# A DeltaNet and mixture-of-experts kernel: PSUM banks by pairs, a short product summed by VectorE, zero fills and gathers moved in the plan

## The chip, the cores and the metric

The kernel runs on one core of a Trainium2 chip. The metric is the device time of one execution in microseconds (us). The engines of the core are TensorE (PE in the profile, PEld for its weight loads), VectorE (DVE), ScalarE (ACT), GpSimd (POOL) and SyncE (SP, which here only issues transfers).

## The reference

Two blocks follow each other. The first is a DeltaNet: for each of 4 x 8 heads a state matrix of 48 x 48 is updated at each of 768 steps. The second routes each of the 3072 rows to one of 8 experts, each of which is a two-layer network.

```python
for t in range(S):                                   # S = 768, per head, D = 48
    y[t] = q[t] @ state
    v_old = k_n[t] @ state                           # k_n is k over its norm
    state = state + b[t] * outer(k_n[t], v[t] - v_old)
x = y.transpose(0, 2, 1, 3).reshape(3072, 384)
expert = argmax(x @ w_gate); gate = softmax(x @ w_gate)[expert]
out[i] = gate[i] * (relu(x[i] @ w1[expert[i]]) @ w2[expert[i]])   # w1 384 x 1024, w2 1024 x 384
```

## The kernel before

**A planner writes the order.** Each operation is registered with `P.op(engine, cost, function, r=, w=, prio=, lat=)`: its engine, an assumed cost in us, the keys that it reads and writes, a priority (smaller first) and, for transfers, an assumed latency. `Plan.order` simulates the engines with these numbers and emits all instructions in the order that it found. On the chip each engine runs its own instructions in that order; the waits between engines are set afterwards, from the tiles that the instructions really read and write. The keys of the planner are its own: PSUM is one key per bank, `("bk", b)`, while the tiles are four pairs of two banks, and bank b lies in pair b // 2.

**The attention** works in 12 chunks (`t`) of 64 steps for all heads. `load_kq(t)` brings keys and queries into a ring of six slots in `kqA`; slots are zeroed first (L332, L1069). `scores(t)` multiplies keys with keys and queries (L373); for t = 0 and 1 the results go by ScalarE (t = 0) and VectorE (t = 1) into `GD` with four copies each (L384 to L388, shown at the helper's lines L307 and L309). `invert(n)` does two chunks at a time on VectorE: two transposes (L436), the norms of the keys (L444 to L466, `nt` at L471), and then a triangular inversion of some hundred small operations. It uses `u` and `x21`, zeroed by GpSimd (L431, L432). `turn(t)` carries the state `S` (two tiles `Sbs`, zeroed at L329), `output(t)` and `logits(t)` make the rows x and their logits, and `route` and `listed` make the lists of rows for each expert (`lst`, `rows_i`) from `ents`, whose first column is a copy of constants from `cf` (L700). `last_rows` zeroes `folds` and writes it to the last rows of `xs`, the buffer of the rows x in device memory.

**The experts.** Each expert takes up to 416 rows: three tiles of 128 and a short one of 32. `early` does the first two tiles of expert 0 before the last rows are known; `expert(e)` does the rest. In each:

- `fetch(e)` gathers rows of `xs` by indirect transfers from GpSimd's queue (L879), `turned_rows` transposes them on TensorE through banks 0 and 1 (L920), and the result is evicted by VectorE (L928) or, for the middle strip, by ScalarE (L926);
- `hidden` makes the hidden layer in eight blocks f of 128 (L938, six instructions each), evicted with a relu by ScalarE for even f (L947) and VectorE for odd f (L944), through the banks given to it;
- `short` makes the second product of the short tile in four column groups (L1015, bank 5), each over two of the eight blocks. ScalarE copies the bank to `folds` (L1019), and `fold` adds the four groups with a matmul against ones (L1023, bank 6);
- `second` makes the second product of a full tile (L967, sixteen instructions), in banks 6, 7 and 5;
- `finish` scales by the gate into one of three `ys` (L955 on VectorE, L958 on ScalarE) and scatters the rows to `out` (L886). All scatters write the key `out`.

What the planner is told sets where the pieces stand: `prio` of transposes is half a step ahead of their expert, so they serve as filling work in the expert before, once their rows are expected to have landed (`lat` of the gather).

## Time and profile before

| | us |
|---|---|
| median of 3 runs (lowest, highest) | 555.9 (553.9, 559.57) |
| the profiled execution | 554.24 |
| its span in the profile | 552.5 |
| TensorE busy in it | 483.8 (88%) |
| VectorE busy | 229.9 (42%) |
| ScalarE busy | 195.5 (35%) |
| GpSimd busy | 84.8 (15%) |
| mean granted clock of TensorE | 0.943 of full |

In the rows of a view, `L967 PE MATMUL pair<-blkA,kqA 128*128 128x384 f32 x32` is line, engine, operation, tile written from tiles read, shape and count; the two numbers ahead of it in a timeline are start and length in us (a merged row has the length from its first start to its last end), and the bracket tells how long the engine had been idle and what it had waited for. Buffer numbers are left out: all four PSUM pairs are called `pair`, and `kqA` in an expert holds gathered rows, transposed rows and hidden layers, since the ring is free by then. fp32 matmuls stand as two instructions each.

### The profile page before, as it was taken

How to read it: one execution, taken by the hardware profiler on the slowest of the kernel's cores; microseconds unless marked ns; L12 is line 12 of the kernel's file. 1: busy time of each engine (PE TensorE's matmuls, PEld its weight loads, DVE VectorE, ACT ScalarE, POOL GpSimd, SP SyncE). 2: the span in 40 equal slices, each digit the busy share in tenths (PEclk: the TensorE clock that was granted, in tenths of full speed). 3: DMA queues.
4: the chain of work that ended last, by engine and by line, in shares of the span. 5: the costliest groups of instructions: out<-in, count | busy, mean ns of one | idle time of the engine just before them, and what ended most of it. 6: DMA issues, size and time to landing. Idle time of an engine off the chain costs nothing. (4 is left out here: it accounts for less than half of the span.)

```text
span 552.5 us, 15891 instructions
## 1 busy us (share of the span) xinstructions
PE 483.8 (88%) x6900; PEld 332.0 (60%) x6901; DVE 229.9 (42%) x932; ACT 195.5 (35%) x459; POOL 84.8 (15%) x91
## 2 busy tenths in 40 slices
PE   5458888778989999898999999999999999999990
PEld 3347777667778889775755555555555555545540
DVE  3999989999899651250211011010110011101100
ACT  3394979778887843410111011011110110111100
POOL 9000000000100001022420142110331102002011
PEclk9557999999999996998999999999999999999995
DMA  8966356464422451393453144412541300001000
GB/s 211 239 158 187 97 162 161 135 162 108 119 95 89 142 199 31 112 386 102 133 200 115 22 171 161 138 50 87 171 163 40 138 2 31 16 0 44 1 30 12
DMA packets 27851, 63.82 MB, mean 116 GB/s; under 512 B 4027, under 2 KB 16221, under 8 KB 27745
## 3 DMA queue, kind: packets, MB, share of 16 engines
q1 hardware_dynamic: 23376, 52.44, 31.4%
q0 software_dynamic: 3584, 9.44, 4.9%
q8 instruction: 55, 0.90, 0.7%
q10 hardware_dynamic: 816, 0.88, 0.7%
q14 instruction: 20, 0.16, 0.1%
HBM read 49.64 MB, written 11.01 MB: 110 GB/s over the span
## 5 line engine op out<-in xcount | busy, mean ns | idle before, releaser
L938 PE MATMUL pair<-kqA,blkA 128*128 128x416 f32 (+2 forms) x288 | 86.3, 457 | 0.4 <-DVE kqA L928 0.4
L967 PE MATMUL pair<-blkA,kqA 128*128 128x384 f32 x240 | 81.0, 495 | 0.0
L944 DVE TENSOR_SCALAR kqA<-pair 128x416 f32<-128x416 f32 (+2 forms) x36 | 19.6, 543 | 127.9 <-PE pair L938 80.1
L938 PEld LDWEIGHTS pair<-kqA,blkA 128*128 128x128 f32 x288 | 51.8, 190 | 32.0 <-issue 29.3
L967 PEld LDWEIGHTS pair<-blkA,kqA 128*128 128x128 f32 x240 | 45.5, 193 | 35.0 <-issue 6.4
L886 POOL DMA_INDIRECT out<-y,rows_i x30 | 28.7, 958 | 201.5 <-ACT y L958 144.6
L947 ACT ACTIVATE kqA<-pair 128x416 f32<-128x416 f32 (+2 forms) x36 | 17.2, 479 | 108.8 <-PE pair L938 79.5
L373 PE MATMUL pair<-kqA 48*64 48x128 f32 (+1 forms) x896 | 35.4, 305 | 20.2 <-ACT pA L307 12.2
L958 ACT ACTIVATE y<-pair,lst 128x384 f32<-128x384 f32 x15 | 8.7, 581 | 124.2 <-PE pair L967 109.5
L938 PE MATMUL pair<-kqA,pA 128*128 128x416 f32 x144 | 51.4, 514 | 0.0
L529 ACT ACTIVATE v<-v,nt 128x48 f32<-128x48 f32 x192 | 48.9, 330 | 1.9 <-DMA v<-in_vtok 1.9
L967 PE MATMUL pair<-pA,kqA 128*128 128x384 f32 x144 | 48.0, 490 | 0.0
L955 DVE TENSOR_SCALAR y<-pair,lst 32x384 f32<-32x384 f32 (+1 forms) x15 | 8.5, 607 | 92.3 <-PE pair L1023 92.3
L373 PEld LDWEIGHTS pair<-kqA 48*64 48x64 f32 x896 | 28.6, 162 | 26.6 <-ACT pA L307 14.1
L938 PEld LDWEIGHTS pair<-kqA,pA 128*128 128x128 f32 x144 | 27.1, 190 | 23.2 <-issue 22.6
L967 PEld LDWEIGHTS pair<-pA,kqA 128*128 128x128 f32 x144 | 26.9, 190 | 21.2 <-issue 3.8
L553 PE MATMUL pair<-S,kqA 112*64 112x96 f32 x704 | 36.1, 255 | 3.4 <-issue 1.6
L879 POOL DMA_INDIRECT kqA<-xs,rows_i x30 | 29.7, 990 | 49.3 <-DMA pA<-in_w 25.5
L553 PEld LDWEIGHTS pair<-S,kqA 112*64 112x64 f32 x704 | 31.4, 141 | 6.1 <-issue 3.8
L582 PE MATMUL pair<-R,blkA 32*32 32x48 f32 x1536 | 28.7, 223 | 4.7 <-ACT R L307 3.3
L582 PEld LDWEIGHTS pair<-R,blkA 32*32 32x32 f32 x1536 | 25.2, 146 | 8.6 <-ACT R L307 4.6
L489 DVE TENSOR_TENSOR prod<-blkA 128x16 f32<-128x16 f32 (+7 forms) x96 | 28.0, 292 | 0.0
(134 smaller groups left out, 628.6 us busy)
## 6 DMA issues: line engine op xcount, KB each, us to landing
kqA<-in_kq SPq DMA_DIRECT2D x46, 192.0 KB, 5.0
blkA<-in_w SPq DMA_DIRECT2D x15, 512.0 KB, 4.7
blkA<-in_w SPq DMA_DIRECT2D x10, 768.0 KB, 5.1
v<-in_vtok SPq DMA_DIRECT2D x12, 384.0 KB, 3.9
kt<-in_ktok SPq DMA_DIRECT2D x12, 384.0 KB, 3.6
xs<-x SPq DMA_DIRECT2D x12, 384.0 KB, 2.8
pA<-in_w SPq DMA_DIRECT2D x9, 512.0 KB, 4.9
pA<-in_w SPq DMA_DIRECT2D x6, 768.0 KB, 5.3
```

Source lines behind the costliest of these rows:

```text
L373: nc.tensor.matmul(bk[bank + e][half(x), i * w : i * w + w].rearrange("p (k c) -> p k c", c=C), lhsT=v[feat(e), 0, x * FQ + f, :], rhs=v[f ...
L489: dve(16 * w, lambda j=j, w=w, pl=pl: nc.vector.tensor_tensor(out=pl, in0=gl[:, 16:32, j : j + 1].to_broadcast([128, 16, w]), in1=u[:, j : ...
L529: P.op("ACT", 0.225, lambda v=v, i=i: nc.scalar.activation(out=v, in_=v, func=AF.Copy, scale=nt[:, 16 * u + i : 16 * u + i + 1]), r=[("nt" ...
L553: nc.tensor.matmul(bk[bank + g][half(x ^ g if first else x), 2 * D * i : 2 * D * i + 2 * D], lhsT=KQ(t)[0 : 64 + D, k, x * FQ + f, :], rhs ...
L582: nc.tensor.matmul(at(BZ, f, e)[quad(q)], lhsT=tt[quad(q), :, 16 * u + 8 * e + f], rhs=R[quad(q), f, e, :], start=True, stop=True, skip_gr ...
L879: nc.gpsimd.indirect_dma_start(out=dst, out_offset=None, in_=xs, in_offset=bass.IndirectOffsetOnAxis(ap=idx, axis=0), bounds_check=N - 1, ...
L886: nc.gpsimd.indirect_dma_start(out=out, out_offset=bass.IndirectOffsetOnAxis(ap=idx, axis=0), in_=src, in_offset=None, bounds_check=N - 1, ...
L938: nc.tensor.matmul(bk[b][:, 0:n], lhsT=a1[:, s, f * 128 : f * 128 + 128], rhs=xT[:, s, :], start=(s == 0), stop=(s == NK - 1))
L944: (lambda f=f, b=b: nc.vector.tensor_scalar(out=hT[:, f, :], in0=bk[b][:, 0:n], scalar1=0.0, scalar2=None, op0=OP.max))
L947: (lambda f=f, b=b: nc.scalar.activation(out=hT[:, f, :], in_=bk[b][:, 0:n], func=AF.Relu)),
L958: (lambda: nc.scalar.activation(out=y[0:n], in_=bk[b][0:n, 0:DM], func=AF.Copy, scale=gate)),
L967: nc.tensor.matmul(bk[b][:, 0:DM], lhsT=hT[:, f, at : at + 128], rhs=a2[:, f, :], start=(f == 0), stop=(f == NF - 1))
```

## The change

The memsets of `Sbs`, of ring slot 0 and of `folds` are registered after the first inversion and read its `nt` in the plan; so do the memsets of `u` and `x21` for the second inversion. The copy into `ents` goes from VectorE to ScalarE, with another priority. The gathers are planned with a latency of 5.0 instead of 2.5 us. `hidden` gets banks that alternate between two pairs, so that ScalarE's blocks lie in one pair and VectorE's in the other, and the second products of a full expert use banks 6, 1 and 7. `short` writes bank 2; the fold and ScalarE's copy are taken out, and VectorE scales the first of the four column groups into y and adds the other three to it, scaled, after which y is scattered at once. The planner then finds another order for the experts' stage.

```diff
-    for i in range(2):
-        P.op("POOL", 1.4, lambda i=i: nc.gpsimd.memset(Sbs[i][:], 0.0), w=[("S", i, e) for e in range(2)], prio=-15)
...
+        past = [("nt", 0)] if n == 1 else []
+        P.op("POOL", 0.9, lambda: nc.gpsimd.memset(u, 0.0), r=past, w=[ku, (*ku, 21)], prio=pr - 1)
+        P.op("POOL", 0.3, lambda: nc.gpsimd.memset(x21[:], 0.0), r=past, w=[kx], prio=pr - 1)
...
-    dve(24, lambda: nc.vector.tensor_copy(out=ents[:, :, 0], in_=const("numbers")), ["cf"], ["ents"], -2)
+    P.op("ACT", 0.15, copy("ACT", ents[:, :, 0], const("numbers")), r=["cf"], w=["ents"], prio=2)
...
-                 r=["rows_i", *allx], w=[("xin", e % 2, t)], prio=30 + e, lat=2.5)
+                 r=["rows_i", *allx], w=[("xin", e % 2, t)], prio=30 + e, lat=5.0)
...
-        hidden(0, xT, hT, 21, guard, (0, 1, 4, 5))
+        hidden(0, xT, hT, 21, guard, (0, 4, 1, 5))
         for t in range(2):
-            second(0, t, hT, 128 * t, 6 + t, 21.2 + 0.01 * t)
+            second(0, t, hT, 128 * t, (6, 3)[t], 21.2 + 0.01 * t)
...
-        hidden(e, xT, hT, pr, guard, (2, 3, 4))
+        hidden(e, xT, hT, pr, guard, (2, 4, 3, 5))
...
-        P.op("PE", 1.6, short, r=hk, w=[("bk", 5)], prio=pr + 0.3, passes=16, use=1536)
-        P.op("ACT", 0.5, lambda: nc.scalar.activation(out=folds[:], in_=bk[5][:, 0:DM], func=AF.Copy),
-             r=[("bk", 5)], w=["folds"], prio=pr)
-
-        def fold():
-            nc.tensor.matmul(bk[6][0:32, 0:DM], lhsT=const("fold"), rhs=folds[:], start=True, stop=True)
+        P.op("PE", 1.6, short, r=hk, w=[("bk", 2)], prio=pr + 0.3, passes=16, use=1536)
...
+        gate, idx = col(3)
+        y, ky = next_y()
+        for c in range(4):
+            part = bk[2][32 * c : 32 * c + 32, 0:DM]
+            P.op("DVE", 0.55, (lambda y=y, part=part: nc.vector.scalar_tensor_tensor(
+                out=y[0:32], in0=part, scalar=gate[0:32], in1=y[0:32], op0=OP.mult, op1=OP.add))
+                if c else (lambda y=y, part=part: nc.vector.tensor_scalar(
+                    out=y[0:32], in0=part, scalar1=gate[0:32], scalar2=None, op0=OP.mult)),
+                r=[("bk", 2), "lst"], w=[ky], prio=pr + 0.35)
+        P.op("POOL", 1.0, lambda y=y: scatter(y[0:32], idx[0:32]), r=[ky, "rows_i"], w=["out"], prio=pr + 0.35, lat=2.5)
+
         for i, t in enumerate(tiles):
-            if i == len(tiles) - 1:
-                P.op("PE", 0.8, fold, r=["folds", "cf"], w=[("bk", 6)], prio=pr + 0.41, passes=2, use=200)
-                gate, idx = col(3)
-                finish(True, 6, 32, gate[0:32], idx[0:32], "rows", pr + 0.4)
-            b = (6, 7, 5)[i]
+            b = (6, 1, 7)[i] if e else 7
             second(e, t, hT, 128 * i, b, pr + 0.4 + 0.01 * i)
             finish(i % 2, b, 128, *col(t), "rows", pr + 0.4)
...
-    last_rows()
...
+            if i == 2:
+
+                for j in range(2):
+                    P.op("POOL", 1.4, lambda j=j: nc.gpsimd.memset(Sbs[j][:], 0.0), r=[("nt", 0)],
+                         w=[("S", j, e) for e in range(2)], prio=-15)
+                P.op("POOL", 1.85, lambda: nc.gpsimd.memset(kqA[:, 0:2048], 0.0), r=[("nt", 0)],
+                     w=kKQ(0) + [("zero", 0)], prio=0)
+                last_rows()
```

## The prediction

> **What bounds the kernel now.** I read the busy rows of the page first: TensorE is busy 88% of the span, no other engine over 42%.

> ```profile
> PE 483.8 (88%) x6900; PEld 332.0 (60%) x6901; DVE 229.9 (42%) x932; ACT 195.5 (35%) x459; POOL 84.8 (15%) x91
> ```

> That is an average over two stages. The table of 25 us windows separates them: from 25 to 175 us VectorE is busy 22.4 to 24.9 us of each 25 (the inversions bound the attention), and from 275 to 525 us TensorE is busy 24.3 to 25.0 of 25 at a granted clock of 1.00. So the head matters through VectorE's chain, the experts through each TensorE instruction and gap, and the last few us through whatever follows the last product. I then read the timeline in four places.

> In an expert (timeline of all engines):

> ```profile
> 447.89 10.59 PE L967 MATMUL pair<-blkA,kqA 128*128 128x384 f32 x32
> 458.52 0.58 ACT L958 ACTIVATE y<-pair,lst 128x384 f32<-128x384 f32 x1 [10.00 <-PE pair L967]
> 459.15 0.83 PE L1023 MATMUL pair<-folds,cf 128*32 128x384 f32 x2 [0.67 <-ACT y L958]
> 459.92 5.43 PE L967 MATMUL pair<-blkA,kqA 128*128 128x384 f32 x16
> ```

> The x32 are two second products, in banks 6 and 7, both in pair 3. ScalarE's y is bank 6's, done half-way, yet it starts after both: an eviction here waits for every earlier write to its pair. The fold wants bank 6, so TensorE waits.

> At the end (same view):

> ```profile
> 535.69 0.98 POOL L886 DMA_INDIRECT out<-y,rows_i  x1 [2.38 <-DMA out<-y,rows_i]
> 538.40 0.58 ACT L958 ACTIVATE y<-pair,lst 128x384 f32<-128x384 f32 x1 [6.33 <-PEq L1112]
> 539.06 0.88 POOL L886 DMA_INDIRECT out<-y,rows_i  x1 [2.40 <-DMA out<-y,rows_i]
> 542.01 0.97 POOL L886 DMA_INDIRECT out<-y,rows_i  x1 [2.07 <-DMA out<-y,rows_i]
> ```

> Scatters run one at a time, each after the transfer of the one before. The last y is ready at 538.98, but the short tile's scatter (0.88) stands ahead of it.

> In the middle, two windows (columns: stretch, its length, busy us of PE, PEld, DVE, ACT, POOL, granted clock, DMA share, GB/s), and from the timeline the wait that they show:

> ```profile
> 248.00:252.00 4.00, 0.89 (x5) 0.78 (x5) 0.42 (x1) 0.39 (x1) 3.08 (x4) 0.87 0.89 305
> 252.00:254.00 2.00, 2.00 (x5) 1.14 (x4) 0.33 (x1) 0.30 (x1) 1.58 (x2) 0.50 0.32 98
> ```
> ```profile
> 251.25 1.09 PE L920 MATMUL pair<-cf,kqA 128*128 128x128 f32 x4 [3.11 <-DMA kqA<-xs,rows_i]
> ```

> TensorE stands 3.11 us for a gather, and then has half its clock for 2 us.

> At the head:

> ```profile
> 6.53 3.44 ACT L307 ACTIVATE blkA<-pair 32x512 f32<-32x512 f32 x5 [2.35 <-PE pair L373]
> 10.34 4.55 DVE L700 COPY ents<-cf 128x24 f32<-128x24 f32 x1 [7.58 <-DMA cf<-c_f]
> 10.43 6.57 DVE L309 COPY blkA<-pair 32x512 f32<-32x512 f32 x4
> 14.44 0.41 POOL L905 MEMSET folds<- 128x384 f32 x1
> 17.11 1.30 DVE L436 STREAM_TRANSPOSE blkA<-blkA 128x512 f32<-128x512 f32 x2
> ```

> VectorE waits for the constants, then a copy of 24 elements takes 4.55 us: it ends at 14.89, when GpSimd's run of zero fills (the last 14.44 + 0.41) is over. The four L309 queue behind it, and L436, first of the inversion, behind them.

> **The change, part by part**, against the profiled execution, 554.24 us (span 552.5 and 1.74 around it).

> *The fold goes.* From the first product's start to the third's is 12.03 us (447.89 to 459.92; 12.02 for experts 5 and 7). The 32 instructions alone are 10.59 − 5.43 = 5.16 us for 16, so 10.32. The fold with its wait costs 1.71 us; in expert 0, where it stands between two hidden chunks, 274.19 to 285.31 is 11.12, less 12 × 0.349 + 5.16: 1.77. Eight experts: 13.7. The fourth L1015 bank now goes to VectorE: one scale and three adds at 0.60 (row of L955 on 32x384), 2.4 us, beside the 5.16 us product that follows, in which VectorE has nothing else. ScalarE loses its folds copy (0.49), hidden before too. **−13.7.**

> *Banks alternate between pairs.* In `hidden` TensorE waits nowhere now (0.4 us in all at L938), so nothing is gained there. The early expert's second product moves to pair 1, which VectorE empties beside the transposes that follow. f and f+2 share a pair, but a chunk lasts 2.1 us (6 × 0.349) and an eviction 0.52 to 0.59: hidden; without that cover each chunk would wait some 0.7. Second products in pairs 3, 0, 3 let the first y start 5.2 us earlier, beside the next product.

> *The transposes move.* In the built order of the changed kernel, four of them stand before each short product instead of eight, and the others gather after the last second product: sixteen before expert 3's hidden, twelve before 5's, eight before 7's. They share pair 0, so a group waits for the evictions of the groups ahead. Two groups, then two L928 (0.59 each) and two hand-overs of 0.1: 1.35 before experts 3 and 5, 0.8 (one eviction) before 7, and about 0.3 before 4 and 6, whose transposed strip ScalarE evicts behind a y (0.58). **+4.1.** Before expert 2 the first two strips' hidden matmuls (1.4 us) cover it. Lower bound 1 (the next strips' matmuls hide most), upper 9 (every group waits for one eviction more).

> *Gathers planned longer.* The early expert's second products now come straight after its hidden product (about 248.2), so 10.3 us of TensorE work covers the gathers, whose last issue was at 252.88. Second products to 258.5, ten transposes with one eviction wait 2.0, then hidden of expert 0, which reaches at 261.1 the place it now has at 265.30. **−4.2**: the 3.1 us wait and 1.1 of half clock. Behind the early scatter POOL now has the second one before expert 2's gathers. Later, gathers stand behind three scatters that wait for y: expert 5's behind expert 2's last. Four gathers at 1.3 each and 4.3 to land, from some 2.3 us after the last product, land 12 us after it; their first reader comes after a whole hidden product (16.8) and waits of 1.3. Cover left: 6 us. SP's order is unchanged; expert 3's weights wait for expert 0's products, which end earlier.

> *Tail.* The short scatter now goes 15 us before the last one, and products are 5.2 apart, over the 3.35 from scatter to scatter. Last y to scatter is 0.27 (532.07 to 532.34), so 539.25 instead of 542.01. **−2.8.**

> *Zeros behind the first logits.* In the built order GpSimd's instructions stand as before and the fills have no wait on nt: the added reads bind the planner alone. SP, whose copy of folds comes behind the fills, keeps its order too. Nothing.

> *ents on ScalarE.* It heads ScalarE's queue and waits for cf (10.34); behind it stand the four L307 copies and the fifth, which ran from 6.53. So: 10.34 + 0.2 + 4 × 0.59 = 12.9 (fifth 13.97; TensorE's next scores and GpSimd's last big fill wait for that, to about 15.2). On VectorE L309 no longer stands behind a copy; its matmuls are done at 7.94 (5.25 + 2.69). Does it run beside the fills? [...] Net 3.6 on VectorE; the ScalarE–TensorE chain gains 2.9 (16.3 for 19.18). Bounds 0 and 4; no row shows a PSUM copy beside a fill, but transposes at 102.17 beside one took their usual 0.70. **−3.3**, passed on, as VectorE bounds the attention.

> Sum: −13.7 + 4.1 − 4.2 − 2.8 − 3.3 = −19.9, so 534.3 on this execution. It stood 1.7 under the median of 555.9; against the median, **536**.

> **Rivals.**
> 1. *The head gives nothing*: L309 stands beside fills, or ScalarE's wait for cf eats it. For: 4.55 us for 24 elements. [...] 539.3.
> 2. *The transposes eat it*: nine evictions' wait, 9 us instead of 4.1. For: pair-wide waits, as in the expert above. Against: the next strip's matmuls. 541. With rival 1, 544.
> 3. *Gathers late (slower)*: POOL's gathers behind scatters land after TensorE wants them; each time costs what it cost at 251 us, 4.2. Six experts: 25, so 561. It decides from gathers 6 us later than reckoned in all six. Against: nothing on POOL grows; the short scatter leaves earlier.
> 4. *The change doesn't do what it says*: true of the zeros, counted at nothing.

> **How the numbers follow.** Forecast 0.68, rival 1 0.12, rival 2 0.10, rival 3 0.06, something that cancels the gain 0.04. The forecast's own range, from head 0 to 4 and transposes 1 to 9, is 532 to 543; with run-to-run spread (553.9 to 559.6) 530 to 544. About 1% (5.6 us) is what can be told from no change. Faster: 0.68 + 0.12 + 0.10, and a part of rival 3 where few gathers are late: 0.92. Same 0.04, slower 0.04.

> **What would show it.** No L1023; VectorE's four operations inside the following product; second products 5.2 apart without gaps. [...] No TensorE wait on a gather, clock 1.00 from 240 on. L920 waits on VectorE of 1 to 1.4 us before experts 3, 5, 7. The last scatter 0.3 behind the last y. I am wrong if L920 waits exceed 9 us, if gathers appear among TensorE's releasers, or if the attention ends no earlier than now.

## The result, and the profile after

| | before | after |
|---|---|---|
| median (lowest to highest), four runs of each | 554.9 us (552.64 to 559.57) | **535.64 us** (532.72 to 541.22) |
| profiled execution, its span | 554.24, 552.5 | 536.05, 534.2 |
| mean granted clock of TensorE | 0.943 | 0.947 |

The ratio is 0.9625, 95% interval 0.9536 to 0.9714. Six more runs beside eleven of before gave medians of 536.96 and 554.44 us, ratio 0.9664 (0.9605 to 0.9723). The ratios leave out disturbed runs, which are not equally many in each set (none of these eleven of before, four of the eleven beside sec5 and the three kernels after it), so that ratios of different sets are not to be held against each other; the medians have all runs in them.

The busy row of the page of the changed kernel: 16 matmul instructions and 8.4 us of TensorE are gone, and VectorE has 12.1 us more, the sums of the short product less what else it no longer does.

```profile
PE 475.4 (89%) x6884; PEld 329.9 (62%) x6885; DVE 242.0 (45%) x955; ACT 191.8 (36%) x452; POOL 84.9 (16%) x91
```

**In an expert** (timeline of all engines but the queues, from expert 5's second products to the start of expert 6; the last row is cut off where the window ends):

```profile
441.92 0.58 ACT L960 ACTIVATE y<-pair,lst 128x384 f32<-128x384 f32 x1 [6.27 <-PE pair L969]
...
447.14 0.62 DVE L957 TENSOR_SCALAR y<-pair,lst 128x384 f32<-128x384 f32 x1 [7.91 <-PE pair L969]
...
452.04 0.60 PE L919 MATMUL pair<-cf,kqA 128*128 128x128 f32 x4
452.29 0.58 ACT L960 ACTIVATE y<-pair,lst 128x384 f32<-128x384 f32 x1 [9.79 <-PE pair L969]
452.48 3.92 PE L937 MATMUL pair<-kqA,blkA 128*128 128x416 f32 x10
```

The three y start 5.2 us apart (441.92, 447.14, 452.29), each as its second product ends; there is no fold between the products.

**The short product and the last scatter** (the same view, expert 7; between the two parts lie the last two products):

```profile
505.33 1.59 PE L1017 MATMUL pair<-pA,kqA 128*32 128x384 f32 x16
505.44 0.59 DVE L943 TENSOR_SCALAR kqA<-pair 128x416 f32<-128x416 f32 x1 [3.60 <-PE pair L937]
506.84 5.43 PE L969 MATMUL pair<-pA,kqA 128*128 128x384 f32 x16
507.01 0.60 DVE L1032 TENSOR_SCALAR y<-pair,lst 32x384 f32<-32x384 f32 x1 [0.98 <-PE pair L1017]
507.65 1.91 DVE L1030 SCALAR_TENSOR_TENSOR y<-pair,lst,y 32x384 f32<-32x384 f32 x3
509.83 0.87 POOL L885 DMA_INDIRECT out<-y,rows_i  x1 [21.07 <-DVE y L1030]
...
522.68 0.58 ACT L960 ACTIVATE y<-pair,lst 128x384 f32<-128x384 f32 x1 [9.79 <-PEq L1121]
523.53 0.98 POOL L885 DMA_INDIRECT out<-y,rows_i  x1 [4.20 <-ACT y L960]
```

VectorE's four operations (0.60 + 1.91) are over at 509.56, when about half of the next product (506.84 to 512.27) is done. The last y is ready at 523.26, its scatter starts at 523.53.

**In the middle** (table of windows: stretch, length, busy us of PE, PEld, DVE, ACT, POOL, granted clock, DMA share, GB/s): TensorE is busy in every us, at full clock, where it had stood 3.1 us.

```profile
248.00:252.00 4.00, 4.00 (x14) 2.41 (x13) 0.00 (x0) 0.58 (x1) 3.06 (x4) 1.00 0.46 144
252.00:254.00 2.00, 2.00 (x8) 1.20 (x7) 0.00 (x0) 0.00 (x1) 1.00 (x1) 1.00 0.53 167
```

**The moved transposes** (timeline of TensorE, ahead of expert 5's hidden product): twelve together; the last four wait for VectorE's evictions.

```profile
415.02 1.04 PE L919 MATMUL pair<-cf,kqA 128*128 128x128 f32 x8
417.24 0.66 PE L919 MATMUL pair<-cf,kqA 128*128 128x128 f32 x4 [1.18 <-DVE kqA L927]
417.74 4.70 PE L937 MATMUL pair<-kqA,blkA 128*128 128x416 f32 x13
```

**At the head** (timeline of the engines):

```profile
8.10 2.79 DVE L309 COPY blkA<-pair 32x512 f32<-32x512 f32 x4 [5.35 <-PE pair L371]
...
10.27 0.22 ACT L307 ACTIVATE ents<-cf 128x24 f32<-128x24 f32 x1 [6.09 <-DMA cf<-c_f]
10.40 4.33 ACT L307 ACTIVATE blkA<-pair 32x512 f32<-32x512 f32 x6
...
12.80 1.30 DVE L435 STREAM_TRANSPOSE blkA<-blkA 128x512 f32<-128x512 f32 x2 [1.91 <-ACT blkA L307]
...
16.70 1.09 DVE L463 TENSOR_SCALAR rt<-rt 128x32 f32<-128x32 f32 x1
17.00 1.98 PE L371 MATMUL pair<-kqA 48*64 48x64 f32 x64 [1.14 <-ACT pA L307]
```

The four L309 run beside GpSimd's fills, which follow each other from 3.66 to 12.73, and take 2.79 us together; the inversion's first transposes start at 12.80 instead of 17.11, nt (18.09) is 3.4 us earlier, and the next scores are 2.2 earlier.

### The profile page after: what moved, and what is told of

It reads as the page before. It is cut to its first block, busy times and chain, and to the rows that moved or that the text cites. A ratio compares the mean times of both kernels' runs of the same rounds, so it can differ in the third digit from the quotient of the medians.

```text
span 534.2 us, 15900 instructions
## 1 busy us (share of the span) xinstructions
PE 475.4 (89%) x6884; PEld 329.9 (62%) x6885; DVE 242.0 (45%) x955; ACT 191.8 (36%) x452; POOL 84.9 (16%) x91
## 3 DMA queue, kind: packets, MB, share of 16 engines
HBM read 49.64 MB, written 11.01 MB: 114 GB/s over the span
## 5 line engine op out<-in xcount | busy, mean ns | idle before, releaser
L969 PE MATMUL pair<-blkA,kqA 128*128 128x384 f32 x240 | 78.9, 488 | 0.0
L943 DVE TENSOR_SCALAR kqA<-pair 128x416 f32<-128x416 f32 (+2 forms) x36 | 19.5, 543 | 124.0 <-PE pair L937 102.6
L371 PE MATMUL pair<-kqA 48*64 48x128 f32 (+1 forms) x896 | 38.2, 323 | 17.0 <-ACT blkA L307 5.8
L371 PEld LDWEIGHTS pair<-kqA 48*64 48x64 f32 x896 | 30.9, 176 | 23.7 <-issue 8.4
L552 PEld LDWEIGHTS pair<-S,kqA 112*64 112x64 f32 x704 | 30.3, 137 | 6.1 <-issue 4.0
L957 DVE TENSOR_SCALAR y<-pair,lst 128x384 f32<-128x384 f32 x7 | 4.3, 618 | 55.3 <-PE pair L969 55.3
```

The costliest lines, as they stand in the source:

```text
L371: nc.tensor.matmul(bk[bank + e][half(x), i * w : i * w + w].rearrange("p (k c) -> p k c", c=C), lhsT=v[feat(e), 0, x * FQ + f, :], rhs=v[f ...
L552: nc.tensor.matmul(bk[bank + g][half(x ^ g if first else x), 2 * D * i : 2 * D * i + 2 * D], lhsT=KQ(t)[0 : 64 + D, k, x * FQ + f, :], rhs ...
L943: (lambda f=f, b=b: nc.vector.tensor_scalar(out=hT[:, f, :], in0=bk[b][:, 0:n], scalar1=0.0, scalar2=None, op0=OP.max))
L969: nc.tensor.matmul(bk[b][:, 0:DM], lhsT=hT[:, f, at : at + 128], rhs=a2[:, f, :], start=(f == 0), stop=(f == NF - 1))
```

## The experiments

Two marks read each profile. **Head and attention**: times from the start, up to the early expert's first hidden product. **Middle and experts**: from that product to the last scatter. The second mark hardly varies (before 306.73 and 307.05 us, after 290.58 and 290.57), the first does.

### The same kernels again, and the head

again_before and again_after are the two kernels unchanged. after_ents_dve and before_ents_act each move one line:

```diff
 after_ents_dve
-    P.op("ACT", 0.15, copy("ACT", ents[:, :, 0], const("numbers")), r=["cf"], w=["ents"], prio=2)
+    dve(24, lambda: nc.vector.tensor_copy(out=ents[:, :, 0], in_=const("numbers")), ["cf"], ["ents"], -2)
 before_ents_act
-    dve(24, ...)
+    P.op("ACT", 0.15, copy("ACT", ents[:, :, 0], const("numbers")), r=["cf"], w=["ents"], prio=2)
```

again_before: 

> The kernel before, profiled once more. The first profile has TensorE at half clock from 206 to 217.6 us and again from 251 to 254.5, and its n-th transposed diagonal (nt) at 21.5, 54.8, 81.4, 107.4, 133.9 and 164.4 us. Theory A (the spells of half clock after 50 us belong to the schedule): the same spells at the same places, nt within 0.3 us of the list. Theory B (a spell is a matter of where a short idle of TensorE falls against something that is not in the schedule): nt 0 and the spell behind the 3.1 us wait at 251 come back, the one at 206 does not, or others appear; marks after 60 us differ by 1 to 4 us between two executions of one kernel.

again_after: 

> The changed kernel, profiled once more. First profile: half clock at 73 to 77.6 and 124.9 to 133.8 us, nt at 18.1, 53.3, 81.5, 107.5, 134.0 and 165.8. Theory A: the same spells. Theory B: nt 0 again at 18.1, spells at other places, so that the attention ends 0 to 5 us earlier than in the first profile. Both: from the hidden product of expert 0 to the end the same within 0.3 us; the ratio of the times near 0.9625.

after_ents_dve: 

> The changed kernel with the copy of ents put back on VectorE, nothing else. The prediction's account: L309 queues behind it until GpSimd's fills pause, the first transposes of the inversion start at about 17.1 instead of 12.8, nt 0 at about 21.5 instead of 18.1, and the attention ends 2 to 3.3 us later (537.5 to 539 us). Rival: the 3.4 us at nt 0 are not what reaches the end of the attention; the stages after 60 us stand where the spells of half clock put them, and the time is within 1.5 us of the changed kernel's, either way.

before_ents_act: 

> The kernel before with the copy of ents on ScalarE, nothing else of the change. The prediction's account: first transposes at 12.8 to 13, nt 0 at 18.1, attention 2 to 3.3 us earlier, 551.5 to 553 us. Rival (rival 1 of the prediction): nothing at the end, 553.5 to 556, because a spell of half clock or another wait takes the lead of the head away before 200 us.

Measured: again_before 553.96 (one run), again_after 536.96, after_ents_dve 538.23, before_ents_act 553.83 us, beside 554.44 of before. In the table, nt is the row named `nt` of each inversion, and the scores are counted by their groups on TensorE. Marks in us; the last column lists the stretches ahead of the early hidden product in which the granted clock is half, without the first one (34 us long in each), worked out from windows of 1 us:

| profile | first transposes | 1st nt | scores, 4th group | 2nd nt | 6th nt | early hidden | at half clock from (for) |
|---|---|---|---|---|---|---|---|
| before | 17.11 | 21.49 | 19.18 | 54.83 | 164.37 | 235.28 | 49 (3.4), 206 (10.2) |
| again_before | 17.11 | 21.49 | 19.18 | 55.63 | 167.32 | 234.37 | 49 (3.4), 76 (3.3), 127 (6.8) |
| before_ents_act | 13.57 | 18.86 | 17.76 | 54.89 | 166.05 | 234.01 | 49, 62, 76, 209 (3.4 each) |
| after | 12.80 | 18.09 | 17.00 | 53.25 | 165.75 | 232.95 | 47 (3.4), 74 (3.4), 125 (6.8) |
| again_after | 12.93 | 18.22 | 17.12 | 53.48 | 163.31 | 235.04 | 73, 97, 141 (3.4 each), 206 (6.8) |
| after_ents_dve | 15.00 | 19.38 | 17.07 | 53.49 | 164.04 | 234.39 | 48, 96 (3.4 each), 205 (10.2) |

Two things follow. First, **the 2nd nt does not follow the 1st**: after_ents_dve is 1.3 us behind the changed kernel at the 1st nt and level with it in the scores, and it is level at the 2nd nt. The timeline of VectorE at the start of the second inversion, in before and then in the changed kernel, shows why:

```profile
52.78 0.71 DVE L436 STREAM_TRANSPOSE blkA<-blkA 128x512 f32<-128x512 f32 x1 [0.39 <-DMA blkA<-blkA]
```
```profile
51.20 0.71 DVE L435 STREAM_TRANSPOSE blkA<-blkA 128x512 f32<-128x512 f32 x1 [2.20 <-DMA blkA<-blkA]
```

In the changed kernel VectorE had been busy until then and had to wait 2.2 us for the diagonals of the next scores, which come by TensorE, ScalarE and a transfer (0.39 before, 1.18 in again_before). A lead of VectorE alone stops there. Nor does a lead of the fourth group of scores reach it whole: before_ents_act is 1.4 us ahead of before in that group, waits 3.04 us at the same row, and has its 2nd nt at 54.89, as late as before.

Second, **stretches at half clock come in lengths of 3.4, 6.8 and 10.2 us, and after 60 us at other places in every execution, of one and the same program too.** The windows of two executions of the kernel before (stretch, length, busy us of PE, granted clock, DMA share, GB/s), the first profile and then again_before:

```profile
125.00:137.50 12.50, 10.38 (x428) 1.00 0.41 103
200.00:212.50 12.50, 11.77 (x283) 0.76 0.28 100
```
```profile
125.00:137.50 12.50, 10.93 (x312) 0.73 0.21 62
200.00:212.50 12.50, 12.00 (x319) 1.00 0.52 175
```

What one costs, in the changed kernel's timeline of TensorE:

```profile
73.07 1.94 PE L371 MATMUL pair<-kqA 48*64 48x128 f32 x32
74.94 2.08 PE L1112 MATMUL pair<-cf 128*128 128x128 f32 x8
76.94 1.48 PE L371 MATMUL pair<-kqA 48*64 48x128 f32 x32
```

In the first profile of before these three took 1.10, 1.16 and 1.10: 2.1 us are lost, the lead of 1.6 us at the 2nd nt is gone at the third (81.48 against 81.36), and a stretch from 125 to 133 makes the changed kernel 1.4 us *later* at the sixth. It then gains, since before has 10 us at half clock from 206 on. The 2.3 us by which the attention ended earlier in the first pair of profiles are therefore not the head's lead carried through. The lengths are one, two and three times 3.4 us, and in before and in the changed kernel the stretches start on a grid of that step (last section). No run moved the grid alone.

after_ents_dve also tells how the copy waits. Its timeline of VectorE and GpSimd:

```profile
10.56 2.21 DVE L699 COPY ents<-cf 128x24 f32<-128x24 f32 x1 [7.81 <-DMA cf<-c_f]
...
12.43 0.30 POOL L431 MEMSET X<- 128x256 f32 x1
12.94 1.81 POOL L1078 MEMSET kqA<- 128x2048 f32 x1 [0.20 <-PE pair L371]
```

The fill at 12.94 came 0.2 us late, and the copy went through in that pause (10.56 + 2.21 = 12.77); in the first profile of before there was no pause until 14.85, and it took 4.55. Neither value that was expected for the first transposes (17.1 or 12.8) came: 15.0. By the medians, the copy's place is worth 0.6 us with the fold (554.44 − 553.83) and 1.3 without (538.23 − 536.96). For the second pair the ratios to before are 0.9664 and, with the copy back, 0.9682 (0.9615 to 0.9749): not told apart. For before_ents_act the ratio is 0.986 (0.9783 to 0.9936), which would be some 8 us, but it rests on the four shortest of eight times that spread from 545.52 to 558.93; the mean of all eight is 0.8 us under that of before. These times tell the copy's worth neither from zero nor from 3.3 us. In before_ents_act's profile TensorE stood 2.05 us ahead of a fold, until ScalarE's late copy to `folds` (276.89), with 3.4 us at half clock after it, and took 309.87 us for the middle and the experts; the other profiles do not have it, and why the copy was late is open.

### Each part of the experts undone

after_fold puts the fold back, the banks staying in pairs (the parts that VectorE sums are taken out):

```diff
+        P.op("ACT", 0.5, lambda: nc.scalar.activation(out=folds[:], in_=bk[2][:, 0:DM], func=AF.Copy),
+             r=[("bk", 2)], w=["folds"], prio=pr)
...
+            if i == len(tiles) - 1:
+                P.op("PE", 0.8, fold, r=["folds", "cf"], w=[("bk", 6)], prio=pr + 0.41, passes=2, use=200)
+                gate, idx = col(3)
+                finish(True, 6, 32, gate[0:32], idx[0:32], "rows", pr + 0.4)
```

> The changed kernel with the fold put back: ScalarE copies the four parts of the short product to folds, TensorE folds them into bank 6 ahead of the last second product, and the short tile's y comes from there; banks alternate between pairs as in the change. Measured from the first hidden product of the early expert to the last scatter (290.6 us in all three profiles of the changed kernel's middle and experts, 306.7 to 307.1 before). The prediction's account (the fold with its wait costs 1.71 us in each expert whatever the banks): 290.6 + 13.7 = 304.3 us. Rival (most of the 1.71 is the wait for a bank whose eviction is held up by the next product's writes to the same pair; with the second product between them in another pair, bank 6 is empty long before): only the two matmuls stay, 0.35 to 0.83 us each, 293.4 to 297.2 us.

Measured: middle and experts **303.63 us**, time 550.39, ratio to before 0.993 (0.9891 to 0.997). That is near the account's 304.3, but by luck: it is made up otherwise. Timeline, expert 5:

```profile
439.49 10.59 PE L969 MATMUL pair<-blkA,kqA 128*128 128x384 f32 x32
...
450.01 0.83 PE L1031 MATMUL pair<-folds,cf 128*32 128x384 f32 x2
450.18 0.62 DVE L957 TENSOR_SCALAR y<-pair,lst 128x384 f32<-128x384 f32 x1 [11.85 <-PE pair L969]
450.77 5.43 PE L969 MATMUL pair<-blkA,kqA 128*128 128x384 f32 x16
```

From the first product to the third it is 11.28 us, less 10.32 for the products: the fold costs 0.96 here, without a wait, not 1.71. The rival was right on that: the other 0.75 goes with the wait for the pair. Of the 13.05 us, 7.7 are eight times 0.96 (taken as alike in all experts); 3.0 are the tail, which the expectation had not counted, where the short tile's scatter again stands ahead of the last one (530.27, 533.87; the last y was ready at 530.61); 1.5 are waits of the following hidden products for ScalarE's evictions behind a late y; 0.9 stay unplaced.

after_oldbanks has VectorE's sum with the banks of before:

```diff
-        hidden(e, xT, hT, pr, guard, (2, 4, 3, 5))
+        hidden(e, xT, hT, pr, guard, (2, 3, 4))
...
-            b = (6, 1, 7)[i] if e else 7
+            b = (6, 7, 5)[i] if e else 6
```

(and 0, 1, 4, 5 for the early hidden product, 6 and 7 for its second ones, 5 for the short one.)

> The changed kernel with the banks of before: hidden products in banks 0, 1, 4, 5 and 2, 3, 4, second products in 6, 7, 5, the short one in 5; the parts still summed by VectorE. In the built order eight transposes stand ahead of each short product again. The prediction's account (alternation gives nothing itself, and brings the moved transposes, some 4 us): from the early expert's first hidden product to the last scatter 286.5 to 287.5 us. Rival (alternation is needed: hidden chunks or second products wait for a pair that is being emptied): 292 us or more, with waits of TensorE on ScalarE or VectorE inside the experts.

Measured: **288.28 us**, 2.3 *less* than with the alternating banks and 0.8 above the account's interval; time 536.71. Expert 7's hidden product starts 3.8 us earlier after the mark (251.76 against 255.52), and no hidden chunk waits. From there to the end it is 1.5 slower, and the timeline of the last microseconds shows the reason:

```profile
517.66 0.58 ACT L960 ACTIVATE y<-pair,lst 128x384 f32<-128x384 f32 x1 [13.61 <-PE pair L969]
...
518.51 0.97 POOL L885 DMA_INDIRECT out<-y,rows_i  x1 [7.61 <-ACT y L960]
521.85 0.97 POOL L885 DMA_INDIRECT out<-y,rows_i  x1 [2.37 <-DMA out<-y,rows_i]
522.87 0.58 ACT L960 ACTIVATE y<-pair,lst 128x384 f32<-128x384 f32 x1 [4.63 <-PEq L1121]
525.19 0.97 POOL L885 DMA_INDIRECT out<-y,rows_i  x1 [2.37 <-DMA out<-y,rows_i]
```

The first y waits for both products in pair 3, so two scatters stand behind each other, 3.34 us apart, and the last waits 1.7 us after its y (523.45).

after_lat plans the gathers at 2.5 us again (`lat=5.0` to `lat=2.5` in `fetch`).

> The changed kernel with the gathers planned at 2.5 us again. Four transposes then stand ahead of the early expert's second products and wait for the gather of tile 2. The prediction's account: TensorE waits 3 us there and has half its clock for some 3.4 us after it, so from the early expert's first hidden product to the last scatter 290.6 + 4.2 = 294.8 us. Rival (something else in the change hides the gather): within 1 us of 290.6.

Measured: **292.82 us**, 2.2 more than with 5.0, and not 4.2; time 539.97, ratio to before 0.9727 (0.9643 to 0.9811). The wait is there:

```profile
251.91 0.63 PE L919 MATMUL pair<-cf,kqA 128*128 128x128 f32 x4 [3.01 <-DMA kqA<-xs,rows_i]
252.38 10.49 PE L969 MATMUL pair<-blkA,kqA 128*128 128x384 f32 x32
```

but this time no half clock came after it (granted clock 1.00 from 248 to 254; 32 instructions of the second product in 10.49 us, 10.59 for expert 5 in before), and the changed kernel pays 0.84 of its own: its ten transposes in one go wait that long for an eviction. Why no half clock came is not shown; the author's reading goes by the grid of 3.413 us (worked out from the starts in the last section): in before, TensorE was busy for only 0.56 us in the stretch of the grid that the wait filled (247.58 to 250.99; again_before 0.39, before_ents_act 0.69), and the half clock began at its end. In after_lat the wait lies, by the same count, across two stretches (247.41 to 250.82 and on to 254.23), with 1.50 and 2.32 us busy, and none began.

### Other banks for transposes and products

tp_pairs puts the transposes in banks 0 and 4 in turn: `b = (0, 4)[s % 2]`.

> The changed kernel with the transposes in banks 0 and 4 in turn instead of 0 and 1, which share a pair. The prediction's account (a group of transposes waits for the evictions of the groups ahead, because they share pair 0; seen: three waits of 1.2, 1.2 and 0.7 us, and some tenths more): from the early expert's first hidden product to the last scatter 287 to 288.5 us. Rival (the waits are for the data of the eviction itself, not for the pair, or the transposes land in pair 2 beside the hidden chunks and wait there): within 0.7 us of 290.6, or more.

Measured: 288.61 us, 2.0 less than the changed kernel and 0.1 outside the account's interval; time 536.76. TensorE's wait for L927 falls from 3.0 to 0.5 us, but six short waits for the last relu in pair 2 (L943, 1.5 us together) come instead, as the rival had it.

sec5 moves the middle second product out of the transposes' pair:

```diff
-            b = (6, 1, 7)[i] if e else 7
+            b = (6, 5, 7)[i] if e else 7
```

> The changed kernel with the middle one of the three second products in bank 5 (pair 2) instead of bank 1, so that only transposes use pair 0. In the built order eight transposes stand ahead of each short product again, and y still leaves pairs 3, 2, 3 in turn. The prediction's account of the moved transposes (3.8 us of waits for pair 0) with the tail kept: from the early expert's first hidden product to the last scatter 286.5 to 287.3 us (290.6 in the changed kernel, 288.3 with the banks of before), no wait of TensorE on VectorE over 0.6 us after 260 us. Rival: the next hidden product, which uses pair 2 second, waits for the middle y: 288 or more.

Measured: **286.08 us**, 4.5 less than the changed kernel and 0.4 under the account's interval; time **531.45**, ratio to before 0.9636 (0.9559 to 0.9714), median of before beside it 553.95. Expert 4's last product and expert 5's hidden one in the timeline of TensorE, to be held against the one shown above:

```profile
407.71 5.32 PE L969 MATMUL pair<-pA,kqA 128*128 128x384 f32 x16
412.87 11.34 PE L937 MATMUL pair<-kqA,blkA 128*128 128x416 f32 x32
```

No transposes are left between them, and nothing waits there; the 0.84 ahead of expert 0's hidden product stays.

### Dummies against the half clock, and a later copy

filler3000 raises the planner's bound on TensorE's dummy matmuls (L1112, whose results nothing reads; `ENOUGH` goes from 2200 to 3000), which makes 116 of 66.

> The changed kernel with the planner's bound on TensorE's dummy matmuls (L1112) raised from 2200 to 3000, which puts 116 of them where there were 66, all before the experts. If a spell of half clock starts because too little went through TensorE in a stretch of some 3.4 us: fewer spells between 55 and 240 us than the 7 to 20 us seen in the profiles of the changed kernel, the sixth nt at 162 to 164, early hidden product at 230 to 233, time 532.5 to 534.5 us and less spread than 531.6 to 539.8. Rival (the dummies fill idle stretches that did not start spells, and each takes a place of 0.25 us on a chain): spells as before, time 536 to 540.

Measured: 536.87 us, lowest 534.92, highest 541.08, ratio to before 0.9736 (0.968 to 0.9793). In the attention its profile has no half clock after 60 us at all, against 10 and 17 us in the two of the changed kernel. The marks of the profile came as expected (6th nt 163.47, early hidden product 232.03, against 232.95 and 235.04), the time did not: it is that of the changed kernel. So the dummies went with a full clock in the one execution seen, and no gain in time is shown.

sec5_ents is sec5 with the copy of ents on VectorE, planned behind the first inversion:

```diff
-    P.op("ACT", 0.15, copy("ACT", ents[:, :, 0], const("numbers")), r=["cf"], w=["ents"], prio=2)
...
             if i == 2:
+                dve(24, lambda: nc.vector.tensor_copy(out=ents[:, :, 0], in_=const("numbers")), ["cf", ("nt", 0)], ["ents"], -2)
```

> The previous kernel but one (middle second product in bank 5) with the copy of ents on VectorE behind nt 0, where nothing of the head waits for it. ScalarE's copies of the first scores then do not wait for the constants: first transposes of the inversion at 11 us instead of 12.9, nt 0 at 16 to 16.5 instead of 18.2, next scores some 2 us earlier. If the lead of the head reaches the end of the attention on average: time 1.5 to 2 us under that of the kernel with bank 5 alone. Rival (spells of half clock decide where the attention ends): within 1 us of it, and an early hidden product anywhere from 230 to 237.

Measured: **529.35 us** (525.94 to 530.67), ratio to before 0.9585 (0.9533 to 0.9636): the lowest median of the study, though the interval overlaps that of sec5. Middle and experts take 286.08 again. The first transposes start at 11.01 as expected, the 1st nt at 17.73 and not at 16 to 16.5:

```profile
12.35 2.53 DVE L443 TENSOR_SCALAR ra<-blkA 128x32 uint32<-128x32 uint32 x1
12.43 0.30 POOL L431 MEMSET X<- 128x256 f32 x1
12.69 1.79 POOL L1078 MEMSET kqA<- 128x2048 f32 x1
...
14.43 0.41 POOL L904 MEMSET folds<- 128x384 f32 x1
```

The next tensor_scalar met the fills, and stood until the last was over (14.84), 2.53 us for 0.19. The fourth group of the next scores starts at 13.08, 4.6 us earlier than in sec5, but then TensorE waits for keys (1.75 us until 17.34), and the last group ahead of the second inversion starts at 44.59, against 44.17 in sec5. The 2nd nt is at 54.53, no earlier than sec5's 54.35, so the 2.1 us between the two medians are not the head's lead at nt; the attention of this profile ended at 231.00, with a single 3.4 us stretch at half clock after 60 us, and what the rest is stays open.

sec5_ents_fill adds the dummies to that.

> All three: middle second product in bank 5, ents copied behind nt 0, bound on dummy matmuls 3000. If the three add: 536 (changed kernel) - 3.7 - 1.9 - 2.5 = 528 us. If only the bank's part is kept: 532 to 533 us.

Measured: 531.41 us, ratio 0.9607 (0.9545 to 0.9669); middle and experts 286.06. Only the bank's part shows; the dummies again show no gain.

## Why the prediction was right, and where it was not

535.64 us was measured for 536 predicted; on the profiled execution 536.05 for 534.3. From the mark to the last scatter the steps without the head sum to −13.7 + 4.1 − 4.2 − 2.8 = −16.6, and −16.2 to −16.5 came. Two more marks in the first pair of profiles, expert 0's short product (272.76 and 266.23) and the end of the last y (538.98 and 523.26), show that the steps hold one by one (us):

| stretch | steps of the prediction | forecast | before | after | measured |
|---|---|---|---|---|---|
| early hidden to expert 0's short product | gathers | −4.2 | 37.48 | 33.27 | −4.2 |
| from there to the end of the last y | fold −13.7, transposes +4.1 | −9.6 | 266.22 | 257.03 | −9.2 |
| from there to the last scatter | tail | −2.8 | 3.03 | 0.27 | −2.8 |

- **Fold, −13.7.** It came. The kernels without the fold and without the moved transposes take 252.65 us (after_oldbanks) and 252.53 us (sec5) for the middle stretch: 13.6 and 13.7 less than before. The prediction had counted the wait with the fold and nothing for the banks, so it did not count the wait twice; 0.75 of the 1.71 is that wait, which alternating banks remove too (after_fold). The two gains do not add.
- **Banks alternating, nothing.** Right for the hidden product: with the banks of before no chunk waits. At the tail alternation is worth 1.5 us.
- **Transposes moved, +4.1.** Right, and place by place: TensorE waits 1.18, 1.18 and 0.69 us for VectorE before experts 3, 5 and 7 (1.35, 1.35 and 0.8 forecast), and the hidden products of experts 4 and 6 take 17.18 us in the changed kernel and 16.93 in sec5 (0.3 each forecast). sec5, which removes what moved them, gains 4.5. Its place (bank 1 in the transposes' pair) was named; that the change would be faster without it was not drawn from it.
- **Gathers, −4.2.** Right against the profile of before, with half clock after the wait. Undone alone (after_lat) the step is worth 2.2, as the half clock did not come: the four transposes and two products behind the wait took 11.1 us there and 12.7 in before, and before waited 0.35 more for an eviction. The wait of 3.0 came in four profiles of four with the short latency, the half clock behind it in three, and it lasts 3.4 us, not 2.
- **Tail, −2.8.** Last y to scatter 3.03 before (538.98, 542.01), 0.27 after.
- **Zeros, nothing.** GpSimd's fills of the head stand in the same order in both profiles, and the last of them starts at 17.69, ahead of nt at 18.09: none waits for it.
- **Head, −3.3: the step that is not borne out.** The 3.6 us for VectorE counted on L309 running beside GpSimd's fills, with a short hold of one tensor_scalar: an estimate that no run had shown. Up to the 1st nt it was close in the changed kernel: beside the fills the four L309 took 0.68 to 0.70 each (0.69 in before, after the fills), the first transposes started at 12.80, when ScalarE's four copies were done (12.9 forecast for these), L463 took 1.09 for 0.18 in before, held 0.9, and 3.4 us were gained for 3.6; the scores gained 2.2 for 2.9. Wrong was "passed on, as VectorE bounds the attention". VectorE is nearly always busy, but the second inversion also had to wait 2.2 us for its scores (the later ones show no such wait). 1.6 us of the lead are left there, and then it lies under differences of 2 to 3 us that executions of one program show. Against 235.28 and 234.37 before, the attention of the changed kernel ended at 232.95 and 235.04. That the first pair of profiles shows 2.3 there is luck of the two executions, and so in part is the closeness of the median: the times tell the head's worth neither from zero nor from 3.3.

The rivals: 1 (the head gives nothing) is not told from the forecast's own head term at the end of the attention; its reasons did not come, as L309 ran beside the fills and the 1st nt gained 3.4 us. 2 and 3 did not come: TensorE waits for no gather in the changed kernel.

## What to carry to other kernels

Ask for each wait that an edit removes whether another part of the same change removes it too, and try the parts alone: here the fold's wait, the banks and the tail were three prices on one pair, and one bank number (1 to 5) was worth another 4.5 us. An engine that is nearly always busy passes a lead on only as far as the first thing it has to wait for: look for the nearest row of the chain beside it. And profile one program twice before a difference of 2 us between two profiles is explained.
